# Attention and routing in other blocks, the first row loads on SyncE's queue, and in chunk 0 the low bits on ScalarE and the leaky relu on VectorE

## Chip, cores and metric

One core of one Trainium2 chip runs the whole program. The metric is device time in microseconds (us) for one execution; the kernel before has been run three times.

## The reference, cut to what matters

```
kv  = einsum('bhsd,bhse->bhde', k, v)          # 8 batches, 8 heads, 576 tokens, 64 wide
x   = einsum('bhsd,bhde->bhse', q, kv)         # no softmax
x   = x / sqrt(mean(x*x, axis=-1) + 1e-6) * g  # then (4608, 512)

h   = x @ w_in                                 # 512 -> 2048, float64 weights
g   = maximum(h, 0) + alpha * minimum(h, 0)    # the leaky relu
x   = g @ w_out                                # 2048 -> 512

logits = x @ w_gate + bias[modality]           # 8 experts
e      = argmax(logits);  gate = softmax(logits)[e]
out    = gate * (relu(x @ w1[e]) @ w2[e])      # 512 -> 1024 -> 512
```

The three stages of float arithmetic are done as sums of rounded parts: a factor is held as a high part (`hi`) and a rest (`lo`), and a product is hi*hi + lo*hi + hi*lo.

## The kernel before, in words

**Phase 1** (attention, dense layers, routing) runs over 12 chunks `c` of 384 tokens (`CT`). A chunk is 16 blocks `s`, one for each 128 of the 2048 hidden columns. In a block TensorE runs `first(c, s)`, 12 matmuls of 128x384 into the PSUM tile `h`, and then `second(c, s-1)`, 9 matmuls of 128x512 into three PSUM tiles `y` that collect over the chunk. Between the two lies the leaky relu: `gg` from `h`, then `ghi` (ScalarE's rounded copy of `gg`), then `glo` (GpSimd, `gg - ghi`). `second` of a block therefore waits for `ghi` and `glo` of that block, which were made while TensorE did the next `first`.

Every engine runs its instructions in the order in which the code issues them. Around `first` and `second` the loop over `c` and `s` puts, by conditions on `s`:

- the attention of the next chunk: `attend` (matmuls), `attended` (copies out of PSUM), `squares` (ScalarE), `rsqrt` (VectorE), then in two blocks `scale_x` and `turn_x` (VectorE: multiply `xs` by the norm, and transpose within 32x32), and at block 15 `take_x`, which makes `xhi` (ScalarE) and `xlo` (VectorE) behind transposes on TensorE (`turn_first`), four of them;
- the routing of the chunk before: `y_out` copies `y` to `yrow` (block 0), `dots` takes 24 dot products per chunk on VectorE (3 token tiles by 8 experts, each over 128x512), `choose`, `weigh`, `count` (two matmuls), `place` (the rows' positions), `scatter` (GpSimd's indirect DMA of `yrow` to `xb` in DRAM, one per tile);
- `pre_load`, `pre_hi` (ScalarE), `pre_lo` (GpSimd, 128x512), `pre_store`: the expert weights are split and stored to `wsp` in DRAM, 128 pieces, 12 blocks of each chunk.

**Chunk 0** also makes `W` out of the float64 weights of both dense layers, which lie there as pairs of int32. They come in 32 halves of 128x512, two to a block and one more in blocks 2 and 4 (`AHEAD`). A half `n` goes through `cut_a` (ScalarE: the high word, scaled, to `wa`), `low_bits` (three bits of the low word), `sign_bit` and `high_bits` (VectorE, bitwise), and then `cut_c` (ScalarE: `hi` rounded into `W`; GpSimd: the rest). `cut()` issues `cut_c(h)`, the bit operations of `h+1` and `cut_a(h+2)`; with `first` as its argument it issues `first` ahead of `cut_a(h+2)`. The bit operations work in `cut_b(n)`, a PSUM bank, `spare`. Its leaky relu is two activations on ScalarE (the positive part, and the negated negative part into `pad`) and one instruction on VectorE.

**The hand-off.** In the last chunk (11) there is no next attention, `dots` takes 4 per block, and `leader()` finds the first item's expert. `load_rows(0..2)` loads rows of the first three items from `xb` (a table entry into a register, four DMAs, and one for `tail`), and `load_expert(0)` loads that expert's weights in two halves of 4096 KB, issued by SyncE; the first half waits until the first rows are there. What is left of the routing of chunk 11's own rows (`dots`, `far_mul` and `far_add` on GpSimd, `choose`, `count`, `place`, `scatter`) is woven into the first items.

**Phase 2** has 41 items (`MAIN`) of 128 rows of one expert: `load_rows`, `turn_rows`, `layer1`, `turn_h`, `layer2`, and an indirect DMA of the result. The first three items (`PLAIN`) turn rows on TensorE, the others with VectorE's 32x32 transposes.

Of the kernel before, what the change touches and what calls it, by code (L numbers as in the profile page):

```python
# [20 lines left out]
D = 512  # L21
# [23 lines left out]
def fused(ctx: ExitStack, tc, qT, kv, g2, wmoe, alpha, wgate, bias, modality, w12, out):  # L45
# [15 lines left out]
    ps_a = phase1.enter_context(tc.tile_pool(name="ps_a", bufs=2, space=PSUM))  # L61
    spare = phase1.enter_context(tc.tile_pool(name="ps_s", bufs=1, space=PSUM)).tile([128, 512], F32, name="spare")
# [9 lines left out]
    nalpha = one.tile([128, NFB], F32, name="nalpha")  # L72
# [30 lines left out]

    def other(n=512):
        return (pools[1] if pools else ps_a).tile([128, n], F32, tag="a", name="a")
# [81 lines left out]
    def cut(later=None, between=None):  # L187
# [3 lines left out]
        steps = [lambda: low_bits(h + 1), lambda: sign_bit(h + 1), lambda: high_bits(h + 1)]  # L191
# [7 lines left out]
        cut_a(h + 2)  # L199
        load_w(h + 7)  # L200
# [133 lines left out]
    def turn_first(k):  # L334
        ps = (other, other, lambda n: spare[:, 0:n], bank)[k](CT)
# [18 lines left out]
    def first(c, fb, between=None):  # L354
# [40 lines left out]
    def y_out(c, t):  # L395
# [62 lines left out]
    def place(c):  # L458
# [294 lines left out]
    with tc.manual_schedule():  # L753
# [183 lines left out]
        for t in (1, 0, 2):  # L937
            y_out(c, t)
# [103 lines left out]
```

## Time and profile before

| what | value |
|---|---|
| three runs | 1442.33, 1443.76, 1447.72 us (median 1443.76) |
| the profiled execution | 1442.01 us, of which the span from first to last instruction is 1440.4 us |
| mean granted clock of TensorE | 0.984 |
| TensorE matmuls busy | 1374.2 us (95%) |
| TensorE weight loads | 1170.0 us (81%), beside the matmuls |
| VectorE | 1084.9 us (75%) |
| GpSimd | 681.6 us (47%) |
| ScalarE | 528.0 us (37%) |

Times of rows count from the span's start. Four stretches are used below: chunk 0 (23.2 to 114.3 us), chunks 1 to 10 (114.3 to 875.7), chunk 11 with the hand-off until the end of the first item's second layer (875.7 to 991.5), and the rest of phase 2. In the rows PE is TensorE, DVE is VectorE, ACT is ScalarE, POOL is GpSimd, SP is SyncE, and SPq its queue. The chain that ended last is no help here: it is the last indirect store alone.

### The profile page before, as it was taken

The page shows a single profiled execution, that of the slowest core. Times are in us where ns is not written, and L with a number is a line of the kernel's source. Part 1 is how long each engine was busy: PE and PEld are TensorE (multiplying, and loading weights), DVE is VectorE, ACT ScalarE, POOL GpSimd, SP SyncE. Part 2 cuts the span into 40 slices and gives each one's busy share as a digit, 9 for nine tenths or more (in the row PEclk, how much of TensorE's full clock was granted, in tenths as well). Part 3 has the DMA queues.
Part 4 walks back from the last instruction along what each step waited for, and adds up shares of the span by engine and source line. Part 5 has one row for each costly group of instructions (what it writes and reads, how often), then busy time and mean ns, then how long its engine had stood idle before and what let it go on. Part 6 is the DMA issues. An engine that isn't in the chain of part 4 may idle for free. (4 is left out here: it accounts for less than half of the span.)

```text
span 1440.4 us, 26864 instructions
## 1 busy us (share of the span) xinstructions
PE 1374.2 (95%) x8878; PEld 1170.0 (81%) x8878; DVE 1084.9 (75%) x2246; ACT 528.0 (37%) x1141; POOL 681.6 (47%) x707
## 2 busy tenths in 40 slices
PE   8889999999999999999999998888999999999997
PEld 7778888888888888978888887766888888888886
DVE  6998887878887787987878879738666666666664
ACT  4663323232322323232233222123454445444543
POOL 2765555545545454645554554654433333333321
PEclk9999999999999999999999999999999999999999
DMA  8855464543546453545454333363721153447784
GB/s 284 267 182 164 159 204 150 194 170 117 166 160 201 143 199 129 173 168 187 150 189 160 132 136 132 127 250 100 297 52 45 52 213 115 162 161 281 289 323 178
DMA packets 80982, 250.71 MB, mean 174 GB/s; under 512 B 12429, under 2 KB 30861, under 8 KB 78672
## 3 DMA queue, kind: packets, MB, share of 16 engines
q1 hardware_dynamic: 68128, 219.25, 43.2%
q0 software_dynamic: 12720, 29.72, 6.6%
q8 instruction: 78, 1.28, 0.4%
q14 instruction: 56, 0.46, 0.1%
HBM read 158.69 MB, written 91.54 MB: 174 GB/s over the span
## 5 line engine op out<-in xcount | busy, mean ns | idle before, releaser
L361 PE MATMUL h<-xhi,W 128*128 128x384 f32 x1536 | 439.3, 347 | 1.3 <-POOL W L185 0.7
L375 POOL TENSOR_TENSOR glo<-gg,ghi 128x384 fp32r<-128x384 f32 x192 | 227.3, 1184 | 399.3 <-ACT ghi L373 374.1
L389 PE MATMUL y<-W,ghi 128*128 128x512 f32 x1152 | 308.3, 403 | 38.8 <-ACT ghi L373 37.4
L361 PEld LDWEIGHTS h<-xhi,W 128*128 128x128 f32 x1536 | 289.3, 193 | 12.8 <-ACT xhi L350 1.4
L389 PEld LDWEIGHTS y<-W,ghi 128*128 128x128 f32 x1152 | 212.6, 189 | 88.4 <-ACT ghi L373 50.8
L408 DVE CUSTOM_DVE_ANT_0 junk<-yrow,wg_sb 128x512 f32<-128x512 f32 x278 | 270.8, 974 | 6.7
L361 PE MATMUL h<-xlo,W 128*128 128x384 f32 x768 | 263.9, 344 | 0.0
L643 PE MATMUL h<-W,xhi 128*128 (+1 forms) x656 | 207.2, 397 | 0.0
L643 PE MATMUL y<-W,hth 128*128 (+1 forms) x656 | 203.9, 392 | 1.3 <-ACT hth L699 1.3
L373 ACT CAST ghi<-gg 128x384 fp32r<-128x384 f32 x192 | 98.4, 513 | 288.1 <-DVE gg L369 216.0
L215 POOL TENSOR_TENSOR raw<-raw 128x512 f32<-128x512 f32 x128 | 197.2, 1541 | 0.5
L368 DVE TENSOR_SCALAR gg<-h,alpha_sb 128x384 f32<-128x384 f32 x176 | 107.2, 609 | 116.6 <-PE h L361 105.9
L389 PE MATMUL y<-W,glo 128*128 128x512 f32 x576 | 168.2, 400 | 6.7 <-POOL glo L375 6.7
L211 ACT CAST raw<-raw 128x512 fp32r<-128x512 f32 x128 | 79.6, 622 | 241.3 <-DMA raw<-in_w_dram 189.1
L719 POOL DMA_INDIRECT out_dram<-kvbd,tail x41 | 42.4, 1034 | 259.3 <-ACT kvbd L717 252.0
L361 PEld LDWEIGHTS h<-xlo,W 128*128 128x128 f32 x768 | 148.2, 193 | 6.8 <-DVE xlo L351 0.2
L643 PEld LDWEIGHTS h<-W,xhi 128*128 128x128 f32 x656 | 123.8, 189 | 29.8
L643 PEld LDWEIGHTS y<-W,hth 128*128 128x128 f32 x656 | 123.4, 189 | 29.8 <-ACT hth L699 1.7
L389 PEld LDWEIGHTS y<-W,glo 128*128 128x128 f32 x576 | 107.5, 189 | 36.3 <-POOL glo L375 11.6
L643 PE MATMUL h<-W,xlo 128*128 (+1 forms) x328 | 130.3, 397 | 2.3 <-DVE xlo L632 2.3
L700 DVE TENSOR_TENSOR htl<-hh,hth 128x512 fp32r<-128x512 f32 x76 | 52.7, 693 | 105.8 <-ACT hth L699 105.8
L679 DVE TENSOR_SCALAR hh<-h 32x256 f32<-32x256 f32 x304 | 126.6, 416 | 6.3 <-PE h L643 1.7
(203 smaller groups left out, 1595.8 us busy)
## 6 DMA issues: line engine op xcount, KB each, us to landing
wsp<-raw SPq DMA_DIRECT2D x128, 512.0 KB, 3.0
W<-wsp SPq DMA_DIRECT2D x16, 4096.0 KB, 13.4
raw<-in_w_dram SPq DMA_DIRECT2D x128, 256.0 KB, 3.3
kvt<-in_kv_dram SPq DMA_DIRECT2D x30, 512.0 KB, 5.2
xs<-xb POOLq DMA_DIRECT2D x164, 64.0 KB
raw<-in_wmoe_dram SPq DMA_DIRECT2D x17, 512.0 KB, 5.3
qT<-in_qT_dram SPq DMA_DIRECT2D x11, 768.0 KB, 6.4
wg_sb<-in_wmoe_dram SPq DMA_DIRECT2D x15, 512.0 KB, 4.6
```

The source lines that it names most:

```text
L211: A.copy(sp_t[n][:, 0:512].bitcast(F32R), sp_t[n][:, 512:1024])
L215: G.tensor_tensor(lo, lo, hi, ALU.subtract)
L361: PE.matmul(ps, w_at(fb, part)[:, k * 128:(k + 1) * 128], x[:, k, :], start=(i == 0), stop=(i == 11))
L368: V.tensor_scalar(gg, ps, 0.0, alpha_sb[:, fb:fb + 1], ALU.min, ALU.mult)
L373: A.copy(ghi, gg)
L375: G.tensor_tensor(glo, gg, ghi.bitcast(F32), ALU.subtract)
L389: PE.matmul(y_t[c][t], a[:, t * 128:(t + 1) * 128], w, start=(fb == i == 0), stop=(fb == NFB - 1 and i == 2))
L408: V.tensor_tensor_reduce(junk, yb_t[c][t][:, 0:D], wg_sb[:, e, :], 1.0, 0.0, ALU.mult, ALU.add, lg_t[c][:, t, e:e + 1])
L643: m = PE.matmul(ps, a, w, start=start, stop=stop)
L679: m = V.tensor_scalar(to, of, 0.0, None, ALU.max) if mine else A.activation(to, of, AF.Relu)
L700: V.tensor_tensor(v, x, u.bitcast(F32), ALU.subtract)
L719: d = G.indirect_dma_start(out=out, out_offset=IndirectOffsetOnAxis(ap=tail[:, i, 1:2].bitcast(I32), axis=0), in_=y, in_offset=None, bound ...
```

## The change

**Chunk 0.** `low_bits` of halves 2 and up is one activation on ScalarE instead of a VectorE instruction (the scale, and a bias of -0.5 from a 128x1 tile `minus`). It is issued right behind `cut_a` of the same half, and so one `cut()` earlier than before; its target is `spare` or a second bank, by turns, save for halves 20 to 28, which all use `spare`. The leaky relu becomes the same two VectorE instructions as in the other chunks.

**Chunks 1 to 10.** The attention of the next chunk lies one block earlier (`attend` from block 8, `scale_x` in blocks 12 and 13). `dots` begins at block 0 (3 in each of blocks 0 to 7), `choose` is in block 7, `count` and `weigh` in 8, `place` in 9, `scatter` in 9 to 11 (before 11 to 13). The split of the expert weights goes to blocks 0 to 11. The positions are cast by one VectorE copy instead of a GpSimd cast for each tile.

**Chunk 11 and the hand-off.** `dots` of chunk 10 takes 3 per block as elsewhere; `leader` and the three scatters are in block 9 (before in block 8), the row loads in block 11 (before 10). `load_rows(i)` for i < 6 is issued by SyncE instead of GpSimd. `dots` of chunk 11 reads `y` in PSUM, and only two of its tiles are copied out ahead of phase 2. The order of the first items is now `turn_rows(1)`, `layer1(0)`, `turn_rows(2)`, `layer1(1)`, `turn_h(0)`, `layer2(0)`.

**Item 40** takes the path of the first three for `layer1` and `turn_h`. The PSUM tiles of attention and `turn_first` are three fixed banks.

```diff
@@ phase 1 tiles
-    ps_a = phase1.enter_context(tc.tile_pool(name="ps_a", bufs=2, space=PSUM))
-    spare = phase1.enter_context(tc.tile_pool(name="ps_s", bufs=1, space=PSUM)).tile([128, 512], F32, name="spare")
+    ps_a = phase1.enter_context(tc.tile_pool(name="ps_a", bufs=1, space=PSUM))
+    banks = [ps_a.tile([128, 512], F32, name=f"bank{i}") for i in range(3)]
+    spare = banks[2]
@@ cutting the float64 weights
-        return (scratch[:, 3072:3584] if n < 2 else spare).bitcast(I32)
+
+        return (scratch[:, 3072 + n * 512:3584 + n * 512] if n < 2 else banks[1] if n % 2 and not 20 <= n < 29 else spare).bitcast(I32)
 
     def low_bits(n):
-        if n < 2 * NFB:
+        if n < 2:
             V.tensor_scalar(cut_b(n).unsqueeze(2), raw_t[n][:, :, 0:1].bitcast(U32), 2.0 ** -29, 7.0, ALU.mult, ALU.min)
+        elif n < 2 * NFB:
+
+            A.activation(cut_b(n).unsqueeze(2), raw_t[n][:, :, 0:1].bitcast(U32), AF.Identity, bias=minus, scale=2.0 ** -29 * (1 - 2.0 ** -22))
...
-        steps = [lambda: low_bits(h + 1), lambda: sign_bit(h + 1), lambda: high_bits(h + 1)]
+        steps = [lambda: sign_bit(h + 1), lambda: high_bits(h + 1)]
         if later is None:
             for step in steps:
                 step()
...
         if between:
             between()
         cut_a(h + 2)
+        low_bits(h + 2)
         load_w(h + 7)
@@ first(c, fb)
-        if c == 0:
-            A.activation(gg, ps, AF.Relu)
-            A.activation(pad[:, 0:CT], ps, AF.Relu, scale=-1.0)
-            V.scalar_tensor_tensor(gg, pad[:, 0:CT], nalpha[:, fb:fb + 1], gg, ALU.mult, ALU.add)
-        else:
-            V.tensor_scalar(gg, ps, 0.0, alpha_sb[:, fb:fb + 1], ALU.min, ALU.mult)
-            V.scalar_tensor_tensor(gg, ps, 0.0, gg, ALU.max, ALU.add)
+        V.tensor_scalar(gg, ps, 0.0, alpha_sb[:, fb:fb + 1], ALU.min, ALU.mult)
+        V.scalar_tensor_tensor(gg, ps, 0.0, gg, ALU.max, ALU.add)
@@ routing
-        if t == 0:
+        if t == 0 and c < NCH - 1:
             V.tensor_copy(y, y_t[c][t])
         else:
             A.copy(y, y_t[c][t])
...
     def dots(c, lo, hi):
         for i in range(lo, hi):
             t, e = divmod(i, E)
-            V.tensor_tensor_reduce(junk, yb_t[c][t][:, 0:D], wg_sb[:, e, :], 1.0, 0.0, ALU.mult, ALU.add, lg_t[c][:, t, e:e + 1])
+            y = y_t[c][t] if c == NCH - 1 else yb_t[c][t][:, 0:D]
+            V.tensor_tensor_reduce(junk, y, wg_sb[:, e, :], 1.0, 0.0, ALU.mult, ALU.add, lg_t[c][:, t, e:e + 1])
...
-        pos_t[c] = pos, mx
+        V.tensor_copy(pos, mx)
+        pos_t[c] = pos
 
     def scatter(c, ts):
-        pos, mx = pos_t[c]
+        pos = pos_t[c]
         for t in ts:
-            G.tensor_copy(pos[:, t:t + 1], mx[:, t:t + 1])
@@ load_rows(i)
-        r = G.value_load(tab, min_val=0, max_val=E * BUCKET + 1024 - 128)
+        q = SP if i < 6 else G
+        r = q.value_load(tab, min_val=0, max_val=E * BUCKET + 1024 - 128)
...
-            d = G.dma_start(to, of)
+            d = q.dma_start(to, of)
         row_dma[:] = [d.ins.name]
-        G.dma_start(tail[:, i, :], src[:, D:D + 2])
+        q.dma_start(tail[:, i, :], src[:, D:D + 2])
@@ layer1(i) and turn_h(i)
+        plain = i < PLAIN or i == MAIN - 1
+        for n in range(2 if plain else 0):
             A.activation(h[:, n].rearrange("p (c b i) -> p b c i", b=4, c=4), pair[:, n].rearrange("p (b c i) -> p b c i", b=4, c=4), AF.Relu)
-        for a in range(0 if i < PLAIN else 4):
+        for a in range(0 if plain else 4):
...
-            if i < PLAIN:
+            if i < PLAIN or i == MAIN - 1:
@@ the loop over chunks c and blocks s
-                    at = AT if c == 0 else 9
+                    at = AT if c == 0 else 8
                     if at < s <= at + 3:
                         squares(nxt, s - at - 1)
                     if at <= s < at + 3:
...
                         rsqrt(nxt, later, s - at - 3)
                     if c > 0 and s == at + 3:
                         rsqrt(nxt)
-                    if s == 13:
+                    if s == at + 4:
                         scale_x(nxt, 0)
                         scale_x(nxt, 1)
                         turn_x(nxt, 0)
-                    if s == 14:
+                    if s == at + 5:
                         scale_x(nxt, 2)
                         turn_x(nxt, 1)
                         turn_x(nxt, 2)
 
                 if c > 0:
-                    per = 3 if nxt < NCH else 4
-                    if 1 <= s <= 24 // per:
-                        dots(c - 1, per * (s - 1), per * s)
-                    if s == 24 // per:
+                    if s < 8:
+                        dots(c - 1, 3 * s, 3 * s + 3)
+                    if s == 7:
                         choose(c - 1)
-                    late = nxt < NCH
-                    if s == 24 // per + 1:
+                    if s == 8:
+                        count(c - 1)
                         weigh(c - 1)
-                    if s == 24 // per + 1 + late:
-                        count(c - 1)
-                    if s == 24 // per + 2 + late:
+                    if s == 9:
                         place(c - 1)
                         if nxt == NCH:
                             leader()
                             scatter(c - 1, range(3))
-                    if nxt < NCH and 11 <= s < 14:
-                        scatter(c - 1, [s - 11])
-                    if nxt == NCH and s == 10:
+                    if nxt < NCH and 9 <= s < 12:
+                        scatter(c - 1, [s - 9])
+                    if nxt == NCH and s == 11:
                         for i in range(3):
                             load_rows(i)
                         load_expert(0)
...
 
                 if c > 0:
-                    if s not in (10, 11, 14, 15):
+                    if s < 12:
@@ between the phases
          c = NCH - 1
-        for t in (1, 0, 2):
-            y_out(c, t)
+        y_out(c, 1)
+        y_out(c, 2)
+        turn_rows(1)
         phase1.close()
         pools.append(ctx.enter_context(tc.tile_pool(name="ps_p", bufs=2, space=PSUM)))
         pools.append(ctx.enter_context(tc.tile_pool(name="ps_o", bufs=1, space=PSUM)))
...
         far_mul(c, 0)
         far_mul(c, 1)
         add(0)
-        dots(c, 0, 7)
+        dots(c, 0, 4)
         layer1(0, lambda: add(1, 2))
-        turn_rows(1)
+        turn_rows(2)
         load_rows(3)
-        dots(c, 7, 8)
+        dots(c, 4, 8)
+        y_out(c, 0)
         add(3, 4)
+        layer1(1, lambda: add(5, 6))
         turn_h(0)
-        add(5)
         dots(c, 16, 22)
-        layer1(1, lambda: add(6, 7))
-        turn_rows(2)
-        add(8, 9)
+        add(7, 8, 9)
         choose(c)
         weigh(c)
         layer2(0, lambda: count(c))

```

In chunk 0 the first place is ScalarE's sequence around two blocks; `wa` is what `cut_a` makes, `wg_sb` and `raw` hold the float64 words, `bank_76` and `bank_77` are the two banks. Before:

```order
L184 CAST W<-wa 128x512
L364 ACTIVATE gg<-h 128x384
L365 ACTIVATE pad<-h 128x384
L373 CAST ghi<-gg 128x384
L157 ACTIVATE wa<-wg_sb 128x512
L184 CAST W<-wa 128x512
L157 ACTIVATE wa<-raw 128x512
```

ScalarE at the same place in the changed kernel, from one `ghi` to the next:

```order
L371 CAST ghi<-gg 128x384
L155 ACTIVATE wa<-wg_sb 128x512
L168 ACTIVATE bank_76<-wg_sb,minus 128x512
L186 CAST W<-wa 128x512
L155 ACTIVATE wa<-wg_sb 128x512
L168 ACTIVATE bank_77<-wg_sb,minus 128x512
L186 CAST W<-wa 128x512
L371 CAST ghi<-gg 128x384
```

The two activations on `h` are gone ahead of `ghi`, and two on the low words stand behind it, each behind the `cut_a` of its half. VectorE in the same blocks of the changed kernel:

```order
L366 TENSOR_SCALAR gg<-h,alpha_sb 128x384
L367 SCALAR_TENSOR_TENSOR gg<-h,gg 128x384
L173 SCALAR_TENSOR_TENSOR bank_76<-raw,bank_76 128x512
L178 SCALAR_TENSOR_TENSOR wa<-wa,bank_76 128x512
L173 SCALAR_TENSOR_TENSOR bank_77<-raw,bank_77 128x512
L178 SCALAR_TENSOR_TENSOR wa<-wa,bank_77 128x512
L366 TENSOR_SCALAR gg<-h,alpha_sb 128x384
```

What moved: VectorE does the sign and the high bits of two halves between two leaky relus, each on a bank that ScalarE has filled, where it did three bit operations of each half before.

At the end of a chunk, VectorE before (`L324` is `scale_x`, `L342` is `turn_x`, `L351` is the `xlo` of `take_x`):

```order
L368 TENSOR_SCALAR gg<-h,alpha_sb 128x384
L369 SCALAR_TENSOR_TENSOR gg<-h,gg 128x384
L324 TENSOR_TENSOR xs<-xs,it 128x512
L342 STREAM_TRANSPOSE xs<-xs 128x512 x2
L368 TENSOR_SCALAR gg<-h,alpha_sb 128x384
L369 SCALAR_TENSOR_TENSOR gg<-h,gg 128x384
L351 SCALAR_TENSOR_TENSOR xlo<-xs,g_sb,xhi 128x384 x4
```

The same end of a chunk in the changed kernel:

```order
L327 TENSOR_TENSOR xs<-xs,it 128x512
L345 STREAM_TRANSPOSE xs<-xs 128x512 x2
L366 TENSOR_SCALAR gg<-h,alpha_sb 128x384
L367 SCALAR_TENSOR_TENSOR gg<-h,gg 128x384
L366 TENSOR_SCALAR gg<-h,alpha_sb 128x384
L367 SCALAR_TENSOR_TENSOR gg<-h,gg 128x384
L354 SCALAR_TENSOR_TENSOR xlo<-xs,g_sb,xhi 128x384 x4
```

What moved: a block with nothing but the leaky relu on VectorE stands between the last transposes and `take_x`. At the start of a chunk VectorE now has, between the leaky relu of block 0 and that of block 1 (`L399` is the copy in `y_out`, `L407` one dot product in two instructions):

```order
L399 COPY yrow<-y 128x512
L407 ISA junk,lg<-yrow,wg_sb 128x512
L407 ISA lg 128x1
L407 ISA junk,lg<-yrow,wg_sb 128x512
L407 ISA lg 128x1
L407 ISA junk,lg<-yrow,wg_sb 128x512
L407 ISA lg 128x1
L366 TENSOR_SCALAR gg<-h,alpha_sb 128x384
```

Before, the copy alone stood there. The row loads, on GpSimd before (behind the last scatter, `L474`; one item's loads are shown):

```order
L474 DMA xb<-yrow,pos 38912x514
L215 TENSOR_TENSOR raw<-raw 128x512
L375 TENSOR_TENSOR glo<-gg,ghi 128x384 x2
L602 TENSOR_LOAD tab_111
L602 ISA x2
L610 ISA
L610 DMA xs<-xb 128x4x32
```

And on SyncE's queue in the changed kernel:

```order
L211 DMA raw<-in_w_dram 128x512
L222 DMA wsp<-raw 128x1024 x2
L602 TENSOR_LOAD tab_110
L602 ISA x2
L610 ISA
L610 DMA xs<-xb 128x4x32
```

What moved: the loads stand behind the last loads and stores of the expert weights' split, on the queue that then issues the first expert's weights, and no `glo` stands behind them.

## Rows read from the trace of the kernel before

**Rows 1.** Busy time by stage: start:end, length, engines (xcount), clock, DMA share, GB/s.

```profile
23.20:114.30 91.10, 79.46 (x606) 64.92 (x607) 85.28 (x139) 62.02 (x129) 57.64 (x49) 0.98 0.62 208
114.30:875.70 761.40, 736.35 (x5781) 647.03 (x5780) 618.82 (x1320) 220.60 (x476) 407.02 (x358) 0.99 0.49 166
875.70:991.50 115.80, 97.21 (x436) 82.14 (x435) 79.20 (x177) 27.03 (x59) 64.73 (x61) 0.93 0.41 146
991.50:1427.60 436.10, 434.82 (x1890) 353.30 (x1888) 287.89 (x572) 211.13 (x463) 148.25 (x231) 1.00 0.51 186
```

The engines stand in the order PE, PE's weight loads, DVE, ACT, POOL.

**Rows 2.** Timeline of DVE in chunk 0: start, duration, instruction.

```profile
28.10 0.61 DVE L366 SCALAR_TENSOR_TENSOR gg<-pad,nalpha,gg 128x384 f32<-128x384 f32 x1
...
67.60 0.61 DVE L366 SCALAR_TENSOR_TENSOR gg<-pad,nalpha,gg 128x384 f32<-128x384 f32 x1
...
71.10 0.70 DVE L171 SCALAR_TENSOR_TENSOR spare<-raw,spare 128x512 int32<-128x512 int32 x1
...
72.50 0.61 DVE L366 SCALAR_TENSOR_TENSOR gg<-pad,nalpha,gg 128x384 f32<-128x384 f32 x1
...
94.61 0.96 DVE L366 SCALAR_TENSOR_TENSOR gg<-pad,nalpha,gg 128x384 f32<-128x384 f32 x1 [0.16 <-ACT pad L365]
```

**Rows 3.** Timeline of ACT in one block of chunk 0.

```profile
68.24 0.51 ACT L373 CAST ghi<-gg 128x384 fp32r<-128x384 f32 x1 [1.87 <-DVE gg L366]
68.66 0.66 ACT L157 ACTIVATE wa<-raw 128x512 f32<-128x512 f32 x1
69.23 0.60 ACT L184 CAST W<-wa 128x512 fp32r<-128x512 f32 x1
69.74 0.67 ACT L157 ACTIVATE wa<-raw 128x512 f32<-128x512 f32 x1
```

**Rows 4.** ACT's groups: count, busy us, mean ns of one, idle before.

```profile
L717 ACT ACTIVATE kvbd<-y,tail 128x512 f32<-128x512 f32 x41 | 28.2, 688 | 96.7 <-PE y L643 96.7
...
L403 ACT COPY yrow<-y 128x512 f32<-128x512 f32 x24 | 13.9, 585 | 46.9 <-PE y L389 46.9
```

**Rows 5.** What PE waited for, chunks 1 to 10: total, times, longest.

```profile
PE y L389 <- ACT ghi L373: 25.0, 21, 2.0
```

**Rows 6.** Timeline of DVE at the end of chunk 4.

```profile
407.57 3.52 DVE L324 TENSOR_TENSOR xs<-xs,it 128x512 f32<-128x512 f32 x1
...
412.24 0.57 DVE L368 TENSOR_SCALAR gg<-h,alpha_sb 128x384 f32<-128x384 f32 x1
```

**Rows 7.** Busy time in a stretch behind it (columns as in Rows 1).

```profile
415.07:418.48 3.41, 3.41 (x11) 3.19 (x10) 1.20 (x2) 0.00 (x0) 0.26 (x1) 0.50 0.60 174
```

**Rows 8.** Timeline of DVE: blocks 6 and 7 of chunk 7, block 1 of chunk 8.

```profile
599.92 0.62 DVE L368 TENSOR_SCALAR gg<-h,alpha_sb 128x384 f32<-128x384 f32 x1 [0.24 <-PE h L361]
...
601.04 0.68 DVE L408 CUSTOM_DVE_ANT_0 junk<-yrow,wg_sb 128x512 f32<-128x512 f32 x1
...
604.13 0.62 DVE L368 TENSOR_SCALAR gg<-h,alpha_sb 128x384 f32<-128x384 f32 x1 [0.24 <-PE h L361]
...
652.10 0.62 DVE L368 TENSOR_SCALAR gg<-h,alpha_sb 128x384 f32<-128x384 f32 x1 [1.00 <-PE h L361]
...
655.60 1.67 DVE L408 CUSTOM_DVE_ANT_0 junk<-yrow,wg_sb 128x512 f32<-128x512 f32 x1
```

**Rows 9.** What PE waited for, last chunk and hand-off.

```profile
PE y L389 <- POOL glo L375: 6.7, 2, 6.3
```

**Rows 10.** Timeline of POOL and of SP's queue at the hand-off.

```profile
927.18 0.98 POOL L474 DMA_INDIRECT xb<-yrow,pos  x1 [0.28 <-POOL pos L473]
...
929.52 0.34 SPq L219 DMA_DIRECT2D wsp<-raw  x1
...
932.58 3.11 POOL L610 DMA_DIRECT2D xs<-xb  x4 [0.88 <-issue]
...
945.64 12.63 SPq L586 DMA_DIRECT2D W<-wsp  x2
```

**Rows 11.** DMA issues, 940 to 960 us: count, KB each, us to landing.

```profile
W<-wsp SPq DMA_DIRECT2D x2, 4096.0 KB, 12.0
```

More of the change, by code (lines that the diff above doesn't have):

```diff
@@ L71, in fused @@
     alpha_sb = one.tile([128, NFB], F32, name="alpha_sb")
-    nalpha = one.tile([128, NFB], F32, name="nalpha")
+    minus = one.tile([128, 1], F32, name="minus")
     g_sb = one.tile([128, 4], F32, name="g_sb")
@@ L102, in bank @@
         return ps_h.tile([128, n], F32, tag="h", name="h")
-    def other(n=512):
-        return (pools[1] if pools else ps_a).tile([128, n], F32, tag="a", name="a")
     four = lambda a: a.rearrange("p (a b) -> p a b", a=4)
@@ L223, in kv_mm @@
         if p == 0:
-            kvps[b] = four(other())
+            kvps[b] = four(banks[0])
         t = kv_t.pop((b, p))
@@ L237, in attend @@
         q = q_t[c]
-        ps = [other(256 * len(ts)).rearrange("p (a b) -> p a b", b=64) for _ in range(2)]
+        ps = [b[:, 0:256 * len(ts)].rearrange("p (a b) -> p a b", b=64) for b in banks[:2]]
         for a in range(4 * len(ts)):
@@ L334, in turn_first @@
     def turn_first(k):
-        ps = (other, other, lambda n: spare[:, 0:n], bank)[k](CT)
+        ps = banks[k][:, 0:CT] if k < 3 else bank(CT)
         for t in range(3):
@@ L452, in count @@
         hot, hb, lg = hot_t[c]
-        ps = (other(48) if pools else spare[:, 0:48]).rearrange("p (n a b) -> p n a b", n=2, a=3)
+        ps = (pools[1].tile([128, 48], F32, name="rps") if pools else spare[:, 0:48]).rearrange("p (n a b) -> p n a b", n=2, a=3)
         PE.matmul(ps[:, 0].rearrange("p a b -> p (a b)"), tri, hb.rearrange("p a b -> p (a b)"), start=True, stop=True)
@@ L609, in load_rows, with turned @@
                 to, of = rows[i][32 * b:32 * b + 32], src[:, 128 * b:128 * b + 128].rearrange("(a j) c -> j a c", j=32)
-            d = G.dma_start(to, of)
+            d = q.dma_start(to, of)
         row_dma[:] = [d.ins.name]
-        G.dma_start(tail[:, i, :], src[:, D:D + 2])
+        q.dma_start(tail[:, i, :], src[:, D:D + 2])
     order = lambda t: t.rearrange("p (c a j) -> p c a j", c=4, a=4)
-    def turned(x):
-        ps = ps_y.tile([128, D], F32, tag="y", name="turned") if pools else other()
+    def turned(x, n_turned=None):
+        ps = ps_y.tile([128, D], F32, tag="y", name="turned") if pools else banks[n_turned]
         for k in range(4):
@@ L629, in turn_rows @@
         if i < PLAIN:
-            ps = turned(flat)
+            ps = turned(flat, i)
             A.copy(hi, ps)
@@ L671, in layer1 @@
                 between()
-        for n in range(2 if i < PLAIN else 0):
+        plain = i < PLAIN or i == MAIN - 1
+        for n in range(2 if plain else 0):
             A.activation(h[:, n].rearrange("p (c b i) -> p b c i", b=4, c=4), pair[:, n].rearrange("p (b c i) -> p b c i", b=4, c=4), AF.Relu)
-        for a in range(0 if i < PLAIN else 4):
+        for a in range(0 if plain else 4):
             for b in range(4):
@@ L769, in fused @@
         V.memset(magic, 0x5F3759DF)
+        V.memset(minus, -0.5)
         V.memset(kvt[64:128, :, 4, :], 0.0)
@@ L780, in fused @@
         warm(WARM[0])
-        ops.extend(four(b) for b in (other(), other(), spare))
+        ops.extend(four(b) for b in banks)
         ms_t[0] = one.tile([128, 24], F32, tag="ms", name="ms")
@@ L817, in fused @@
         high_bits(1)
-        V.tensor_scalar(nalpha, alpha_sb, -1.0, None, ALU.mult)
         cut_a(2)
+        low_bits(2)
         load_w(6)
```

## The prediction, as written before the run

> **What bounds the kernel now.** I read the busy time of each engine by stage first, because the average (TensorE 95% busy) hides where it waits. In phase 2 behind the first item TensorE is busy 434.82 of 436.10 us at the full clock [rows 1]: nothing that the change moves there can give anything back, and the stage stays. What can be won or lost lies in the other three stretches. In chunk 0 VectorE is the fullest engine, 85.28 of 91.10 us, and TensorE has 11.6 us idle. In chunks 1 to 10 TensorE idles 25 us, and the list of its waits puts all of it down to one releaser, `ghi`, in 21 waits [rows 1, 5]. In chunk 11 with the hand-off it idles 18.6 us of 115.8 and the granted clock is 0.93 [rows 1].
>
> Then I read the timelines to see what is late at each of these waits. The block pitch where TensorE sets it is 4.21 us, from one leaky relu to the next that starts as soon as `h` is there [rows 8].
>
> **The change, part by part.**
>
> **Chunk 0.** Today VectorE paces it: the leaky relus of an ordinary block stand 4.90 us apart (67.60 to 72.50), while ScalarE waits 1.87 us for `gg` ahead of its `ghi` [rows 2, 3]. The change takes two `low_bits` and the single-instruction leaky relu from VectorE and gives it the two-instruction one, so VectorE's own work falls by about 0.8 us a block. But the order on ScalarE now closes a loop. `ghi` needs the leaky relu; behind `ghi` stand, in this order, `cut_a`, `low_bits`, `cut_c`, `cut_a`, `low_bits`; the second `low_bits` feeds `sign_bit` and `high_bits`, and behind these VectorE does the next leaky relu. Before, VectorE made the low bits itself, ahead of that point, and nothing of this was serial. I add the loop up from starts. `ghi` to `cut_a` 0.42, `cut_a` to what follows 0.57, `cut_c` to `cut_a` 0.51 [rows 3]. For the new `low_bits` no row exists. It is an activation of 128x512 like `cut_a` (0.66), plus an operand from a column: the one activation of that size with such an operand takes 0.688 from PSUM against 0.585 for the plain copy from PSUM [rows 4], so I add 0.10 and take 0.77, starting the next thing 0.67 later. Then: 0.42 + 0.57 + 0.67 + 0.51 + 0.57 + 0.77 = 3.51 from `ghi` to the end of the second `low_bits`; 1.40 for sign and high bits (71.10 to 72.50) [rows 2]; about 1.21 for the leaky relu of two instructions (1.12 to the start of the next instruction, and the overlap) [rows 8]; and 0.06 for two hand-overs. That is 6.18 us a block against 4.90.
>
> A third half in the block (blocks 2 and 4) adds 0.51 + 0.57 + 0.67 = 1.75, so 7.93. Where one bank serves both halves (20 to 28, some four blocks) the second `low_bits` must also wait until VectorE has read the first, 0.57 more: 6.75. For twelve blocks, with 0.67 for the block that also copies the kv product: 6 x 6.18 + 0.67 + 2 x 7.93 + 4 x 6.75 = 80.6 us, and I see 66.5 today (28.10 to 94.61) [rows 2]. That is +14.1, and about 1 more in the last blocks: **+15 us**. From below: a `low_bits` that is as short as `cut_a` takes 0.1 twice out of the loop, some 3 us of the chunk, and if the hand-overs overlap too some 9 are left; from above, if TensorE's clock fell in the gaps, a stretch at half clock costs 1.7 (below), but 4.21 + 1.7 = 5.9 is still inside 6.18, so it would hide. Between +9 and +20.
>
> The Trainium skill's page "ScalarE: Activation LUTs", section "What ACT_TABLE_LOAD costs", gives 186 ns plus 0.833 ns for each column, 93 ns for each column operand, and an overlap of 93 ns between activations. That makes 0.706 us for `low_bits`, a block of about 6.06 and an estimate of +13.4 for the chunk; the row's `cut_a` at 0.66 is already above the page's 0.61, and my sum goes by the rows.
>
> **Chunks 1 to 10.** The long wait comes at each chunk's end. `scale_x` on VectorE takes 3.52 us instead of the 0.6 of its twins, since GpSimd is then in the scatter, the split's subtraction and `glo`; so the leaky relu of block 15 starts at 412.24, some 2.3 after its `h` [rows 6]. In the change `scale_x` comes in blocks 12 and 13, where GpSimd has neither scatter nor split, and a block with the leaky relu alone lies between. I take out the 25.0 [rows 5] and put back 0.45 a chunk for the two blocks with transposes: -20.5. Behind these waits the clock falls: 3.41 us at 0.50 [rows 7], in six of the ten chunks, 1.7 lost each; these go with the wait: -10.
>
> New is block 0: leaky relu, copy, and three dots. A dot alone takes 0.68, beside GpSimd up to 1.67 [rows 8]. VectorE has 1.00 us of slack ahead of the leaky relu of block 1 [rows 8]; three dots with their accumulator reads, two of them blocked, are 4.0 to 4.3, so it comes 3.3 late. `ghi` is due one pitch, 4.2, after `h`, and leaky relu and `ghi` take 1.9 to 2.0 of it, so 2.2 are forgiven: 1.1 us of wait a chunk, **+11**. The following groups of three keep up: between 599.92 and 604.13 VectorE does leaky relu and three dots and still waits 0.24 for `h` [rows 8], so the backlog clears. Sum **-20 us**, between -30 (block 0 costs nothing) and -8 (block 0 costs double).
>
> **Chunk 11 and the hand-off.** What can be won at most is TensorE's idle, 115.8 - 97.2 = 18.6, and what the clock takes: 0.93 mean means some 16 us at half clock, 8 lost. Together 26.6. The largest single wait is 6.3 for a `glo` [rows 9], which stands on GpSimd behind the row loads that it issues from 932.58 to 944.4 [rows 10]; on SyncE's queue these block no engine that computes. What stays or comes new is the first expert's first half. Today the last scatter ends 52.5 after the chunk's start (875.7), and the half is issued at +69.9 and lands 12.0 later, +81.9 [rows 10, 11]. In the change block 9 begins at about +41; `place` takes about 3 and three scatters 4.5, so the last one ends at +48.6, and 2 later it is in DRAM. Then 15 loads on SyncE: one issue costs 0.34 there at least (the split's store) and 0.78 if as on GpSimd (3.11 for four) [rows 10]; at the middle, 0.56, and with the table reads, they are done at +59.5, landed by +61.7, and the half is there at +73.7. TensorE has 16 blocks of 4.21 plus 3.3 of waits behind it at +70.7, so it waits about 3. Also left: about 4 for `count` of chunk 11, whose last dots now stand behind `turn_h(0)`, and 1.1 in block 1. 26.6 - 8.1 = 18.5, so **-18 us**; between -12 (loads at 0.78, a clock fall stays) and -23.
>
> One rule speaks to the dots from PSUM. The Trainium skill's page "SBUF — State Buffer", section "Who interferes with whom", says that a VectorE instruction with two SBUF inputs contends with a GpSimd instruction that reads SBUF, and that one with at most one SBUF input does not. This trace agrees: 0.68 free, 1.67 beside GpSimd, both inputs in SBUF [rows 8]; by the page the 14 dots of chunk 11 are safe, while those moved into block 0 are not.
>
> `load_rows(4)` and `(5)`, item 40 and the single copy of the positions lie beside a TensorE that is busy throughout [rows 1]; uncovered, they could cost some tenths each, and I put them at nothing.
>
> **The sum.** 1442.0 + 15 - 20 - 18 = 1419 against the profiled execution. The median of the runs lies 1.75 above that execution, so the forecast is 1420 us.
>
> **The rivals.** First, the chunk's end doesn't give: another VectorE stall takes the place of `scale_x`, or the leaky relu is late by the backlog of dots, and the 21 waits and the six clock falls stay. For it speaks that every instruction there with two SBUF inputs can meet a `glo`; against it, that only the one beside scatter and split is long. 1442 + 15 + 11 - 18 + 1.75 = 1452, or 1441 if the dots of block 0 fit: about no measurable change.
>
> Second, slower: the dot groups don't clear. If each group of three went like the first, 5.2 us from leaky relu to the next (652.10 to 655.60 + 1.67) [rows 8] against the pitch of 4.21, eight groups lose 1.0 each, 8 a chunk instead of 1.1, +6.9 x 11 = 76: 1496. It decides from some 2.9 us more a chunk. Against it: groups in the same chunk that do fit [rows 8].
>
> Third, chunk 0 does not lose: ScalarE runs ahead of VectorE by more than I count, so that TensorE's pitch sets the blocks. Then it ends between no loss and 14 gained (16 x 4.8): 1391 to 1405. For it speaks that VectorE's own work falls; against it, the order of the queue, in which the second `low_bits` can't pass `ghi`.
>
> **How the numbers follow.** My case 0.72, with 1406 to 1434 as its own range; the first rival 0.10, the second 0.07, the third 0.11. Half a per cent (7.2 us) is about what a measurement of this kernel can tell from no change; that makes 1436.5 to 1451 "the same". My case and the third rival are faster, but for 0.01 at my case's upper end: 0.82. Same 0.11, slower 0.07. The range, 1399 to 1438, leaves out the first and second rival's times and half of the third's, about 0.2.
>
> **What would show it.** Chunk 0 right: ScalarE without an idle stretch between `ghi` and the second `low_bits`, VectorE waiting for `low_bits`, leaky relus 6.2 apart, the stage about 106 us. Chunks 1 to 10 right: `scale_x` under 1 us, waits for `ghi` gone at block 15 and new at block 1, no stretch at 0.50, a stage of some 741 us. Hand-off right: no wait for a `glo`, half 0 issued near +62, the stage near 98 us. It is wrong if the `low_bits` takes much under or over 0.77, if leaky relus in blocks 1 to 8 start over 4.3 apart throughout, or if SyncE's loads take a microsecond each.

## The result and the profile after

The changed kernel takes 1431.28 us (median of four runs, 1430.04 to 1432.62) against 1444.45 for the kernel before: a ratio of 0.9907, with an interval of 0.9886 to 0.9928. That is inside the predicted range and faster, as forecast, but 11 us above the 1420 that I gave. The profiled execution has a span of 1429.4 us, 11.0 less than before. One run of the kernel with the leaky relu ahead of the bits (below) took 1890.43 us at a granted clock of 0.655 and is left out of that kernel's figures.

The busy time by stage, cut at the same places as in [rows 1] (start of chunks 0, 1 and 11, end of the first item's second layer, TensorE's last wait), with the same columns:

```profile
23.00:132.40 109.40, 84.40 (x606) 68.02 (x607) 75.09 (x124) 68.28 (x127) 58.62 (x50) 0.94 0.53 176
132.40:875.00 742.60, 730.42 (x5781) 639.40 (x5780) 586.79 (x1328) 219.53 (x476) 399.04 (x326) 1.00 0.51 169
875.00:978.04 103.04, 93.31 (x437) 80.41 (x436) 64.57 (x171) 27.03 (x60) 48.91 (x38) 0.93 0.48 164
978.04:1416.50 438.46, 438.13 (x1897) 354.13 (x1895) 284.65 (x569) 209.38 (x458) 143.17 (x218) 1.00 0.51 185
```

Against [rows 1] the four stages moved by +18.3, -18.8, -12.8 and +2.4, which sum to -10.9. Forecast were +15, -20, -18 and nothing. So the terms are off by 3.3, 1.2, 5.2 and 2.4 us, all to the slow side, 12.1 together.

**Chunk 0.** ScalarE between two `ghi`, then VectorE in the same block (start, duration, instruction):

```profile
75.83 0.51 ACT L371 CAST ghi<-gg 128x384 fp32r<-128x384 f32 x1 [2.62 <-DVE gg L367]
76.24 0.66 ACT L155 ACTIVATE wa<-raw 128x512 f32<-128x512 f32 x1
76.81 0.70 ACT L168 ACTIVATE bank<-raw,minus 128x512 int32<-128x512 uint32 x1
77.46 0.60 ACT L186 CAST W<-wa 128x512 fp32r<-128x512 f32 x1
77.97 0.67 ACT L155 ACTIVATE wa<-raw 128x512 f32<-128x512 f32 x1
78.54 0.72 ACT L168 ACTIVATE bank<-raw,minus 128x512 int32<-128x512 uint32 x1
...
81.98 0.51 ACT L371 CAST ghi<-gg 128x384 fp32r<-128x384 f32 x1 [2.18 <-DVE gg L367]
```

```profile
74.59 0.61 DVE L366 TENSOR_SCALAR gg<-h,alpha_sb 128x384 f32<-128x384 f32 x1
...
77.55 0.70 DVE L173 SCALAR_TENSOR_TENSOR bank<-raw,bank 128x512 int32<-128x512 int32 x1 [1.76 <-ACT bank L168]
...
79.29 0.70 DVE L173 SCALAR_TENSOR_TENSOR bank<-raw,bank 128x512 int32<-128x512 int32 x1 [0.25 <-ACT bank L168]
80.09 0.69 DVE L178 SCALAR_TENSOR_TENSOR wa<-wa,bank 128x512 int32<-128x512 int32 x1
80.69 0.61 DVE L366 TENSOR_SCALAR gg<-h,alpha_sb 128x384 f32<-128x384 f32 x1
```

Neither engine is full, and each waits for the other in every block (over the chunk VectorE 26.9 us for the low bits, ScalarE 27.4 for the leaky relu): that is how a loop across two queues reads. Leaky relus stand 6.10 us apart (forecast 6.18), and a `low_bits` takes 0.70 to 0.72 (forecast 0.77).

**Chunks 1 to 10.** What TensorE waited for (total, times, longest), and the group of `scale_x`:

```profile
PE y L387 <- ACT ghi L371: 11.5, 20, 1.3
```

```profile
L327 DVE TENSOR_TENSOR xs<-xs,it 128x512 f32<-128x512 f32 x30 | 29.1, 997 | 0.0
```

The wait was 25.0 in [rows 5], and the granted clock of the stage is now 1.00. The mean of `scale_x` is 1.0 us; before it was 1.6:

```profile
L324 DVE TENSOR_TENSOR xs<-xs,it 128x512 f32<-128x512 f32 x30 | 48.0, 1628 | 0.0
```

In the kernel before, one `scale_x` in each of the ten chunks took 3.5 us. The one in [rows 6], from 407.57 to 411.09, stands beside the third scatter, the split's subtraction and then this `glo` of GpSimd:

```profile
409.51 1.02 POOL L375 TENSOR_TENSOR glo<-gg,ghi 128x384 fp32r<-128x384 f32 x1
```

It ends 0.56 us behind that `glo`, and 0.55 or 0.56 behind it in all ten chunks. In the changed kernel the median is short, but not the longest (ns, least, median and most; three of the 33 lie beside chunk 0):

```profile
L327 DVE TENSOR_TENSOR xs<-xs,it x33: 677/682/2711, 121.3 to 865.0; 128x512 f32<-128x512 f32 x33
```

Seven of the thirty in this stage, in six chunks, still take 1.1 to 2.7 us, each beside a scatter, a subtraction or a `glo`, since GpSimd comes to them late. In five of these six chunks TensorE has no wait for `ghi` at the chunk's end even so. It is argued from the order, and was not tried apart, that the block with the leaky relu alone takes the delay up.

**Chunk 11 and the hand-off.** TensorE's waits from 875 to 985 us, and then the stage in two parts (split where the last dense matmuls end) and the two stretches behind the two large waits:

```profile
PE y L643 <- DVE htl L695: 5.0, 1, 5.0
PE h L643 <- DMA W<-wsp: 3.9, 1, 3.9
```

```profile
875.00:945.00 70.00, 69.17 (x346) 61.59 (x346) 49.52 (x117) 14.36 (x28) 36.50 (x28) 1.00 0.48 154
945.00:978.04 33.04, 24.14 (x93) 18.82 (x91) 15.05 (x54) 12.67 (x32) 12.41 (x10) 0.79 0.46 183
949.72:954.50 4.78, 4.78 (x11) 3.77 (x12) 0.54 (x2) 0.59 (x2) 2.31 (x2) 0.50 0.88 326
969.75:974.90 5.15, 5.15 (x12) 4.08 (x13) 4.84 (x15) 1.67 (x6) 1.28 (x1) 0.50 0.00 0
```

Chunk 11 itself has hardly a gap left, 69.17 of 70.00 us busy. Nearly all loss stands in the 33 us behind it: the wait for the first half of the weights, which was forecast, one for `htl` of the first item, which was not, and behind each of them about 5 us at a granted clock of 0.50, which cost 2.4 and 2.6 us. The wait of 6.3 for a `glo` in [rows 9] is gone.

### The profile page after: what moved, and what is told of

The parts are those of the page before. It is cut to its first block, busy times and chain, and to the rows that moved or that the text cites. A ratio compares the mean times of both kernels' runs of the same rounds, so it can differ in the third digit from the quotient of the medians.

```text
span 1429.4 us, 26802 instructions
## 1 busy us (share of the span) xinstructions
PE 1372.8 (96%) x8886; PEld 1164.7 (81%) x8886; DVE 1024.1 (72%) x2233; ACT 531.3 (37%) x1134; POOL 653.8 (46%) x641
## 5 line engine op out<-in xcount | busy, mean ns | idle before, releaser
L364 PE MATMUL h<-xhi,W 128*128 128x384 f32 x1536 | 432.3, 342 | 2.4 <-POOL W L187 1.9
L364 PEld LDWEIGHTS h<-xhi,W 128*128 128x128 f32 x1536 | 282.1, 188 | 14.2 <-POOL W L187 3.2
L364 PE MATMUL h<-xlo,W 128*128 128x384 f32 x768 | 259.5, 339 | 0.0
L407 DVE CUSTOM_DVE_ANT_0 junk<-yrow,wg_sb 128x512 f32<-128x512 f32 x264 | 243.9, 924 | 6.7
L371 ACT CAST ghi<-gg 128x384 fp32r<-128x384 f32 x192 | 98.2, 512 | 275.9 <-DVE gg L367 228.6
L366 DVE TENSOR_SCALAR gg<-h,alpha_sb 128x384 f32<-128x384 f32 x192 | 117.0, 609 | 111.6 <-PE h L364 109.1
L364 PEld LDWEIGHTS h<-xlo,W 128*128 128x128 f32 x768 | 144.8, 189 | 6.9 <-DVE xlo L354 0.2
L643 PE MATMUL y<-W,htl 128*128 (+1 forms) x328 | 130.8, 399 | 0.0
L680 DVE TENSOR_SCALAR hh<-h 32x256 f32<-32x256 f32 x296 | 123.3, 417 | 4.6
```

The costliest lines, as they stand in the source:

```text
L364: PE.matmul(ps, w_at(fb, part)[:, k * 128:(k + 1) * 128], x[:, k, :], start=(i == 0), stop=(i == 11))
L371: A.copy(ghi, gg)
L407: V.tensor_tensor_reduce(junk, y, wg_sb[:, e, :], 1.0, 0.0, ALU.mult, ALU.add, lg_t[c][:, t, e:e + 1])
L643: m = PE.matmul(ps, a, w, start=start, stop=stop)
L680: m = V.tensor_scalar(to, of, 0.0, None, ALU.max) if mine else A.activation(to, of, AF.Relu)
```

## The experiments

Times are medians against the kernel before, run on the same chip in each group.

**Chunk 0 as before, the rest as changed** (1410.85 us, ratio 0.9762, 0.9745 to 0.9778).

```diff
 cut():   steps = low_bits(h+1), sign_bit(h+1), high_bits(h+1)   # all on VectorE, in spare
 first(): if c == 0: two activations and one VectorE instruction
-minus = one.tile([128, 1], F32)
+nalpha = one.tile([128, NFB], F32)
```

> The changed kernel with chunk 0 as before: low bits on VectorE in one PSUM bank, leaky relu with two activations on ScalarE. Theory (the order on ScalarE closes a loop from one leaky relu to the next and costs 18 us in chunk 0): the stage of chunk 0 goes from 109 back to 91 us, the kernel to about 1413. Rival (the chunk is longer for another reason, such as the fixed PSUM banks or the attention's place): the stage stays above 100, the kernel at 1425 or more. Beside it: an item of phase 2 takes 11.09 us in the kernel before and 11.16 in the changed one; if that comes from the code of phase 2 it is 11.16 here.

```profile
23.20:114.30 91.10, 77.95 (x606) 63.62 (x607) 85.28 (x139) 61.97 (x129) 57.49 (x49) 1.00 0.63 208
```

The stage is back at 91.10, so the edits to chunk 0 cost 18.3 us, and the whole kernel gains 20.4. The 2 us beyond the stage come from phase 2, which went back to the pitch of before; that was not expected (below).

**Only the moved blocks, on the kernel before** (1426.15, ratio 0.9866, 0.985 to 0.9883).

```diff
-at = AT if c == 0 else 9
+at = AT if c == 0 else 8          # scale_x, turn_x at at+4, at+5
-dots in blocks 1..8, scatter in 11..13, pre_* not in 10, 11, 14, 15
+dots in blocks 0..7, scatter in 9..11, pre_* in 0..11      # chunks 1 to 10 alone
```

> The kernel before with only the blocks of attention, routing and weight split in chunks 1 to 10 as in the change (the last chunk's routing as before). Theory (scale_x no longer meets scatter and weight split, and its lateness no longer reaches the wait for ghi at the chunk's end): chunks 1 to 10 go from 761 to about 743 us, no stretch at half clock at the chunk ends, the kernel to about 1425. Rival (the fixed PSUM banks or the single copy of the positions give the gain): over 755 us, 1438 or more. Item of phase 2: 11.09 us.

```profile
114.30:861.40 747.10, 731.42 (x5781) 639.21 (x5780) 587.63 (x1319) 219.98 (x476) 404.64 (x358) 1.00 0.50 169
```

```profile
PE y L389 <- ACT ghi L373: 12.9, 21, 1.6
```

```profile
L324 DVE TENSOR_TENSOR xs<-xs,it 128x512 f32<-128x512 f32 x30 | 28.7, 984 | 0.0
```

`scale_x` is as short as in the changed kernel (0.98 us on the mean), the wait falls from 25.0 to 12.9, the clock stands at 1.00, and the stage is 14.3 shorter, somewhat less than expected (743). Five of the thirty `scale_x` are still long here too, up to 3.2 us. The 4.5 us that the stage lacks against the changed kernel came with its other edits, among them the fixed banks and the single copy of the positions, which were not tried apart.

**Only the row loads on SyncE's queue, on the kernel before** (1431.93, ratio 0.9908, 0.9892 to 0.9925).

```diff
+q = SP if i < 6 else G
-r = G.value_load(...);  G.dma_start(...)
+r = q.value_load(...);  q.dma_start(...)
```

> The kernel before with only the row loads of items 0 to 5 on SyncE's queue. Theory (the glo behind the row loads is the largest wait of the hand-off): TensorE's wait of 6.3 us for glo goes, and the clock fall behind it; what comes is a wait for the first half of the first expert, which lands about where it did, so 4 to 7 us are won: 1438 to 1440. Rival (the hand-off is gained by the order of the first items and by the dots from PSUM): within 2 us of the kernel before. Item of phase 2: 11.09 us.

```profile
877.10:956.10 79.00, 72.19 (x345) 62.59 (x344) 52.37 (x116) 14.75 (x28) 36.19 (x31) 0.98 0.47 157
956.10:981.30 25.20, 21.32 (x92) 16.28 (x92) 23.78 (x53) 12.09 (x31) 16.17 (x10) 0.93 0.46 178
```

12.6 us, about twice what I expected of it: the wait for the first half, which I had set against the gain, did not come. To the end of the first item's second layer this kernel needs 104.2 us, 11.6 less than before: nearly all that the whole change wins there (12.8). The rows show where the rest went: the changed kernel's chunk 11 is 9 us shorter (70.0 against 79.0), but what follows is 8 longer (33.0 against 25.2).

**The leaky relu ahead of the bits** (the changed kernel; 1411.36, the median of three runs, ratio 0.9761, 0.9742 to 0.9781).

```diff
         cut_c(h)
+        if between:
+            between()                 # first(c, s): leaky relu, ghi
         sign_bit(h + 1); high_bits(h + 1)
-        if between:
-            between()
         cut_a(h + 2); low_bits(h + 2)
```

> The changed kernel with one thing moved in chunk 0: first, with its leaky relu and ghi, is issued ahead of sign_bit and high_bits of the block's first half, so that the leaky relu no longer stands behind the bits that need the block before's second low_bits. Durations and counts are the same. Theory (the order's loop costs, not ScalarE's work): leaky relus about 4.3 to 4.6 us apart, the stage of chunk 0 at 78 to 86 us instead of 109, the kernel at 1401 to 1409. Rival (the activations themselves are too much for ScalarE, or the bits are late for W): the stage stays above 100 us, the kernel above 1424.

```profile
31.56 0.61 DVE L366 TENSOR_SCALAR gg<-h,alpha_sb 128x384 f32<-128x384 f32 x1
35.94 0.61 DVE L366 TENSOR_SCALAR gg<-h,alpha_sb 128x384 f32<-128x384 f32 x1
...
95.14 0.61 DVE L366 TENSOR_SCALAR gg<-h,alpha_sb 128x384 f32<-128x384 f32 x1
104.38 0.57 DVE L366 TENSOR_SCALAR gg<-h,alpha_sb 128x384 f32<-128x384 f32 x1
```

The same instructions in another order: 4.38 us a block instead of 6.10, the stage 88.1 instead of 109.4. So it is the order, and not ScalarE's added work. It stays above the 78 to 86 that I expected because not every block is as short: 6.18 us with a third half (35.94 to 42.12), and at worst 9.24 between the leaky relus of blocks 13 and 14, where the bits, the end of rsqrt, `scale_x` and a transpose stand ahead of the second on VectorE.

**`minus` 64 bytes wide** (the changed kernel; 1427.56, ratio 0.988, 0.9857 to 0.9902).

```diff
-minus = one.tile([128, 1], F32, name="minus")
+minus = one.tile([128, 16], F32, name="minus")[:, 0:1]
```

> The changed kernel with one edit: the tile minus is declared 128x16 and its first column is used, so that the tiles declared behind it lie in SBUF where they lay in the kernel before (nalpha was 128x16). The instructions are the same. Theory (the items of phase 2 take 11.16 us instead of 11.09 because every tile behind a 4-byte tile lies off a 64-byte boundary; with chunk 0 as before, and nalpha back, they took 11.09): 11.09 us an item, phase 2 shorter by 2.7 us, the kernel at about 1428. Rival (the pitch comes from the order of chunk 0's instructions or their number): 11.16, 1431.

The activation that writes an item's result, 32 of them in phase 2 (duration, first and last start), in the changed kernel and then with the wider tile:

```profile
L718 ACT ACTIVATE kvbd<-y,tail x32: 688/688/688, 1047.1 to 1393.0; 128x512 f32<-128x512 f32 x32
```

```profile
L718 ACT ACTIVATE kvbd<-y,tail x32: 687/687/688, 1045.8 to 1389.7; 128x512 f32<-128x512 f32 x32
```

Over 31 items that is (1393.0 - 1047.1) / 31 = 11.16 us an item, and (1389.7 - 1045.8) / 31 = 11.09. Not one instruction differs.

**`turn_h(0)` first** (the changed kernel; 1423.9, ratio 0.9867, 0.984 to 0.9893).

```diff
-dots(c, 0, 4); layer1(0, ...); turn_rows(2); dots(c, 4, 8); y_out(c, 0); add(3, 4); layer1(1, ...); turn_h(0)
+dots(c, 0, 8); y_out(c, 0); layer1(0, ...); turn_rows(2); turn_h(0); add(3, 4); layer1(1, ...)
```

> The changed kernel with the first items in another order: all eight dots of the first tile and its copy ahead of layer1(0), turn_h(0) ahead of layer1(1), the sums 3 and 4 behind turn_h(0). Theory (the wait of 5.0 us for htl at layer2(0) comes from ScalarE's queue, in which hth of item 0 stands behind the copy of y, the sums and item 1's relu): the wait goes, and the clock fall behind it (2.5), for about 1 us of wait at turn_h(0): 1425. Rival (it turns into a wait for the relu, for xlo or for count as large): 1429 or more.

Why `htl` was late shows on ScalarE in the changed kernel:

```profile
963.00 0.59 ACT L401 COPY yrow<-y 128x512 f32<-128x512 f32 x1 [3.56 <-DVE lg L407]
...
965.58 0.63 ACT L416 ACTIVATE kvbd<-kvbd 128x512 f32<-128x512 f32 x1 [0.76 <-POOL kvbd L411]
...
967.43 1.06 ACT L675 ACTIVATE hh<-h 128x512 f32<-128x512 f32 x2
968.39 1.07 ACT L694 CAST hth<-turned 128x512 fp32r<-128x512 f32 x2
```

`hth` stands behind item 1's relu, that behind the sums, those behind GpSimd's products, and all behind a copy of `y` that waits 3.56 for the dots. In the new order the wait of 5.0 is gone, that for the first half stays (4.2), the largest new ones are 1.3 (`count`) and 1.0, and the stage to the end of the item's second layer is 98.2 us instead of 103.0:

```profile
872.10:970.28 98.18, 90.43 (x436) 78.07 (x435) 64.43 (x169) 27.04 (x60) 48.61 (x38) 0.98 0.50 172
```

**Half 0 behind two items' rows** (the changed kernel; 1425.04, ratio 0.9866, 0.9841 to 0.9891).

```diff
-for i in range(3): load_rows(i)
-load_expert(0)
+load_rows(0); load_rows(1); load_expert(0, (0,)); load_rows(2); load_expert(0, (1,))
```

> The changed kernel with the first half of the first expert issued behind the row loads of items 0 and 1, and those of item 2 behind it. Theory (SyncE's 15 loads of 10 us set when the half is issued): it is issued some 4 us sooner, lands at about +71 of the chunk instead of +74.7, TensorE's wait of 3.9 and the clock fall behind it go: 1425 to 1427. Rival (the half is paced by its transfer or by rows landing, or item 2's rows and the second half come late in turn): 1430 or more.

SyncE's queue in the changed kernel, and then here:

```profile
926.01 2.15 SPq L610 DMA_DIRECT2D xs<-xb  x4
...
937.64 12.57 SPq L585 DMA_DIRECT2D W<-wsp  x2
```

```profile
933.72 0.36 SPq L585 DMA_DIRECT2D W<-wsp  x1
946.76 3.24 SPq L610 DMA_DIRECT2D xs<-xb  x4
```

The half leaves at 58.8 of the chunk instead of 62.6, TensorE's wait for it goes (1.7 for `xlo` stands there), that of 5.0 for `htl` stays, and the stage falls to 98.3, though item 2's rows now go out 13 us later than the half:

```profile
874.90:973.19 98.29, 90.28 (x436) 78.07 (x435) 64.28 (x169) 27.03 (x60) 48.77 (x38) 0.98 0.50 171
```

**All together** (1400.19, ratio 0.9685, 0.9657 to 0.9713).

```diff
+the four edits above, and in rsqrt's second part: all its steps, then the bits
```

> All together: leaky relu ahead of the bits in chunk 0, minus 64 bytes wide, turn_h(0) first, half 0 behind two items' rows, and in block 13 of chunk 0 the remaining rsqrt steps ahead of the bits instead of woven between. If the gains add: 1431 - 19 - 2.7 - 6 - 5 - 1.5 = 1397. If the waits of the hand-off hide each other, 1403 or more.

```profile
23.10:111.00 87.90, 80.61 (x606) 67.07 (x607) 73.25 (x124) 68.25 (x127) 57.79 (x50) 0.94 0.66 219
111.00:854.10 743.10, 729.39 (x5781) 638.18 (x5780) 581.34 (x1328) 219.04 (x476) 399.65 (x326) 1.00 0.51 169
854.10:951.15 97.05, 90.34 (x437) 78.09 (x435) 64.39 (x169) 26.92 (x60) 48.92 (x38) 0.98 0.51 174
```

Three per cent below the kernel before, and between the two times that I had expected. The two mends of the hand-off hide each other: 97.05 together, 98.2 and 98.3 alone. In all three TensorE is busy 90.3 to 90.4 us at a clock of 0.98: a stretch at half clock stays in each, and with both mends there are new waits of up to 1.8 us. The step moved in rsqrt brought nothing that shows (87.9 against 88.1).

**Dots from block 1 again** (on the kernel just above; 1406.07, ratio 0.974, 0.9724 to 0.9757).

```diff
-dots in blocks 0..7, choose 7, count 8, place 9, scatter 9..11     # chunks 1 to 10
+dots in blocks 1..8, choose 8, count 9, place 10, scatter 10..12
```

> The mended kernel of the run before (about 1400 us) with the dot products of chunks 1 to 10 in blocks 1 to 8 again, choose, count, place and the scatters one block later; chunk 11 as it is. Theory (three dots behind block 0's copy make the leaky relu of block 1 late, which costs 0.7 to 1.1 us of wait a chunk): the waits for ghi in block 2 go, 7 to 10 us less: 1390 to 1393. Rival (the third scatter meets scale_x in block 12 and costs as much, or the backlog only moves): 1398 or more.

Part of the rows were routed elsewhere in this kernel, and why is not known. So its whole time shows nothing, and only the stages ahead of phase 2 are compared.

```profile
PE y L388 <- ACT ghi L372: 15.7, 11, 1.7
PE bank L454 <- DVE hb L435: 6.7, 10, 1.5
```

The rival's outcome came, with another instruction as its victim: no `scale_x` takes over 0.69 us here. The wait of 0.5 us in block 2, which nine of the ten chunks had, went, but chunks 1 to 10 took 749.3 us instead of 743.1. New waits stand at `count` and, 1.3 to 1.7 us each, in block 13. GpSimd and VectorE ahead of one of the latter:

```profile
391.65 0.99 POOL L474 DMA_INDIRECT xb<-yrow,pos  x1 [0.16 <-PE h L365]
392.67 1.31 POOL L218 TENSOR_TENSOR raw<-raw 128x512 f32<-128x512 f32 x1
```

```profile
392.00 2.03 DVE L310 SCALAR_TENSOR_TENSOR it<-u,it 128x24 f32<-128x24 f32 x1
394.06 0.18 DVE L308 TENSOR_TENSOR u<-it 128x24 f32<-128x24 f32 x1
```

A step of rsqrt over 24 elements takes 2.03 us instead of 0.18, and ends as GpSimd's subtraction ends (392.67 + 1.31 = 393.98). Moved by one block, the second scatter and the split fall on rsqrt.

**Attention of chunk 1 one block earlier** (on the mended kernel; 1398.43, ratio 0.9688, 0.9672 to 0.9705).

```diff
-AT = 9
+AT = 8                                   # and halves 18 to 26 in one bank
```

> The mended kernel with the attention of chunk 1, beside chunk 0, one block earlier (from block 8), as in the other chunks. Theory (the stretch from 94 to 103 us, where the bits of two halves, the rest of rsqrt and scale_x stand in one row ahead of a leaky relu, is what keeps chunk 0 at 88 us): the leaky relu of block 14 comes without them, 3 to 5 us less: chunk 0 at 83 to 85 us, 1395 to 1397. Rival (the row only moves a block ahead and costs the same there): 87 us or more, 1399 or more.

```profile
23.00:110.10 87.10, 78.16 (x605) 64.98 (x606) 74.03 (x124) 68.07 (x127) 57.65 (x50) 0.98 0.65 217
```

Chunk 0 is 0.8 us shorter and the kernel within the spread of the one before it: the row of work only moved, with 8.32 us between two leaky relus from 89.81 to 98.13.

## Why the prediction was right, and where its terms were off

The measured time lies in the upper part of the range, since the four misses all lie on the slow side; none made up for another.

**What bounds each stage** held in chunks 1 to 10 (`ghi`) and in the hand-off (waits and clock). That VectorE paced chunk 0 is not shown: in the reordered kernel it has 10.6 us less to do there (74.64 for 85.28), and the stage is 3.0 shorter.

**Chunk 0** was right in its mechanism, and the reordered kernel shows it apart from ScalarE's load. Its twelve counted blocks took 80.4 us (27.11 to 107.48) where I had added up 80.6. The Trainium skill's page "ScalarE: Activation LUTs", section "What ACT_TABLE_LOAD costs", gives by its figures an estimate of 0.706 us for `low_bits`; measured were 0.70 to 0.72, nearer than my 0.77. Mis-sized is "about 1 more in the last blocks": in blocks 12 to 15 the stall for `low_bits` and the steps of rsqrt and `scale_x` come one after the other, and behind a wait of 4.7 the granted clock is 0.50 from 126 to 132 us. All that lies outside the twelve blocks grew by some 4.4 us instead of 1 (18.3 less 13.9).

**Chunks 1 to 10** came within 1.2 us (-18.8 for -20). The step that the rest hangs on, that GpSimd's scatter and split make `scale_x` long, stands in all ten chunks of the kernel before, and the run that moved the scatters by one block shows the same hold on a step of rsqrt. The run with the blocks alone shows that their places give 14.3 of the 18.8. That GpSimd has neither scatter nor split beside `scale_x` any more was wrong in six chunks, and did little harm. Within the stage the parts were off against each other: waits left 11.5 (I counted 4.5 + 11 = 15.5), and TensorE's busy time, in which the clock falls stood, fell by 5.9 and not by 10. Block 0's three dots cost 0.52 in nine of the chunks, 4.7 in all and not 11; 2.8 stand at the chunk's end, and 4.0 in blocks 5 and 6, where I had counted none.

**Chunk 11 and the hand-off** is where the prediction failed, by 5 us (-12.8 for -18). The step was "26.6 - 8.1": I let all of the clock's 8 us go with the old waits and counted the new ones at their length alone. TensorE's idle time fell by 8.9 us (18.6 to 9.7) where I had counted 10.5, and its busy time, in which the clock falls stand, by 3.9 and not by 8. The wait for the half was 3.9 for a forecast 3, landing at +74.7 for +73.7; the one forecast for `count` did not come there, but one of 5.0 for `htl` did, which I had not seen in the order of ScalarE's queue. Each brought a stretch at half clock of its own, 2 x 2.5 us. With the two waits mended, the stage took 97.05; the forecast's figure was near 98. The dots that read `y` in PSUM came out as forecast, 0.69 us each, though four of them lie beside GpSimd's products:

```profile
L407 DVE CUSTOM_DVE_ANT_0 junk<-y,wg_sb 128x512 f32<-128x512 f32 x14 | 9.6, 689 | 0.4
```

**At nothing** I had put phase 2. It lost 2.4 us, 0.07 an item, which the wider `minus` gives back: it comes from where the tiles lie in SBUF.

The first, second and third rivals did not come: the long waits at the chunk's end went, the dots clear but for the 4.0 us above, and chunk 0 lost time. The third has its truth in the reordered kernel, in which ScalarE does run ahead: VectorE waits 7.8 us for the low bits instead of 26.9. Its "16 x 4.8" stands in no row; TensorE's busy time before, 79.46 us, is 4.97 a block.

## What to carry to other kernels

Before work moves to an idle engine, write its queue down from one consumer to the next and add up the path that crosses to the other engine and back: here the idle engine had room, and the order alone cost 21 us. Here a new wait of 4 or 5 us cost its length and some 2.5 us at half clock behind it, so price both. Where one engine's instructions grow long beside another's, as VectorE's beside GpSimd's here, place each by what the other does in the same block, small instructions included.

## What was not expected of the hardware

Two kernels with the same instructions and another width of a 4-byte column, declared among the first tiles of SBUF, differ by 0.6% in phase 2: 11.16 and 11.09 us an item, where TensorE is busy without a break. All kernels here with 64 bytes in that place have 11.09, the changed kernel and the three that keep the 4 bytes 11.16. Which of the tiles behind it counts, and what address would do, was not tried.
